# A GEGLU feed-forward kernel on one core: second-half data staged in single steps, x stored later, GpSimd held once

The change has five parts: sums of w_down staged by single steps with T2 in T1's place, x slices stored later, the first weight sums of the second half kept in the wd ring (with GpSimd held back once), two more warm-up matmuls, and the B21 loads called during M6.

## The chip, the cores and the metric

One core of one Trainium2 chip. The metric is the device time of one execution in microseconds (us), lower is better.

## The reference, cut to what matters

```python
# B, S, D, F = 1, 2048, 1024, 3584; all bf16
def reference(x, w_gate, w_up, w_down):
    return (gelu_tanh(x @ w_gate) * (x @ w_up)) @ w_down
```

## The kernel before

The rows of x are worked in two halves of 1024. Every 2x2 block product is done by a scheme with seven products in place of eight (M1 to M7), which needs sums of blocks: S sums of the left and T sums of the right operand. In the gate and up stage a "pair" (two chunks of 128 hidden columns, gate and up) takes 7 x 2 x 4 = 56 matmuls of 128x512. GpSimd makes the S sums for the next pair, ScalarE moves PSUM banks and does the gelu, VectorE adds M5 to other banks (`add_m5`), multiplies gate and up, and in the first half also does staging work: it makes T2 and T4 of w_down and SyncE stores them in HBM (`t_dram`), since there is room for only a part of them. SyncE also transposes slices of the second half's x and stores them in HBM (`x_dram`). All of these lie in order on their engines' queues.

```python
wd_pool = tile_pool("wd", bufs=3)     # w_down rows, later B21
o_pool  = tile_pool("o",  bufs=4)     # staging sums, x slices, gelu and output tiles

def stage_sums(i):                    # behind M4, for one or two i per pair
    w = staged[i]
    tt = [o_pool.tile([P, DN], F32R, name="o_sb") for _ in range(3)]   # T1, T2, T4
    for t, (in0, in1) in zip(tt, ops):
        dve(nc.vector.tensor_tensor(out=t[:], in0=in0, in1=in1, op=ALU.subtract))
    for j in range(2):                # store T2 and T4
        sp(nc.sync.dma_start(out=t_dram[:, j, i, :], in_=tt[1 + j][:].bitcast(F32)))

def stage_x(tb, kd):                  # behind M5, twice per pair, pairs 2 to 9
    t = o_pool.tile([P, 1, TB], BF16, name="o_sb")
    sp(nc.sync.dma_start_transpose(out=t[:], in_=xv[t0 : t0 + TB, kd : kd + 1, :]))
    sp(nc.sync.dma_start(out=x_dram[:, kd : kd + 1, ...], in_=t[:]))
...  # order inside a pair: M1, M5, M6, M2, M7, M3, M4; `then[...]` runs behind a product
    at = [min((pair - first_pair + d) * 4 // 3, NS) for d in range(3)]
    then["m5"] = [lambda q=q: stage_x(*q) for q in xs[:2]]
    then["m2"] = [lambda i=i: stage_load(i) for i in range(at[1], at[2])]
    then["m4"] = [lambda i=i: stage_sums(i) for i in range(at[0], at[1])]
...  # end of the first half: sums for the second half's first pair, on VectorE
    then1["m3"] = [t_sum("t1"), s_fill(0, "s1", "s2"), s_fill(1, "s1", "s2")]
    then1["m4"] = [a22 (ScalarE), b22 (ScalarE), t_sum("t2"), t_sum("t3"),
                   s_fill(0, "s3"), s_fill(1, "s3"), s_fill(0, "s4"), s_fill(1, "s4"),
                   t_sum("t4"), ...]                                   # shortened
```

## Time and profile before

| | before |
|---|---|
| median of the first three runs, us | 550.91 (550.12 to 553.39) |
| profiled run: whole, span, us | 554.47, 552.7 |
| TensorE busy | 539.6 us, 98% of the span |
| longest waits of TensorE | 4.4 and 1.4 us, both for VectorE's m5 addition |

TensorE is the bound and is almost never idle, so the table is read for what is left: two gaps. The prediction shows the lines. One more view: the waits of SyncE in the first half (who waited, for what: us in total, times, longest).

```profile
SPq L568 <- DMA o_sb<-in_x_dram: 43.1, 16, 6.4
SPq L553 <- DVE o_sb L549: 35.3, 17, 10.3
```
Line 568 is the store of an x slice, and its wait is for the slice's transpose to land: SyncE stood still for it 16 times, 43.1 us in all. Line 553 is the store of a T sum.

### The profile page before, as it was taken

Reading aid. Unit: us, or ns where it says so; the run is one execution under the profiler, and the core shown is the slowest. Engines: PE = TensorE matmul, PEld = TensorE weight load, DVE = VectorE, ACT = ScalarE, POOL = GpSimd, SP = SyncE. Lnnn points to the kernel's source line nnn. Section 1 sums busy time; section 2 is a strip of 40 time slices with the busy share of each in tenths; the row PEclk is TensorE's granted clock in tenths of the full one; section 3 lists DMA queues with packets and bytes.
Section 4 is the critical chain, followed back from the end, with each engine's and each line's share of the span. In section 5 each row is a group of like instructions: output and inputs, shape, how many; then the busy total and the mean of one; then the engine's idle time right before and its main releaser. Section 6 shows DMA issues by size and latency. Waiting matters only on the chain.

```text
span 552.7 us, 7222 instructions
## 1 busy us (share of the span) xinstructions
PE 539.6 (98%) x2373; PEld 375.9 (68%) x2409; DVE 355.1 (64%) x465; ACT 259.3 (47%) x434; POOL 243.0 (44%) x206
## 2 busy tenths in 40 slices
PE   8999999988999999999998999999999999999997
PEld 4457677755777767768676777766777676866765
DVE  0735677567686799789396444444444459979851
ACT  2425554444545516414564455555555552462270
POOL 0367777784778100000038677776777730000000
PEclk9999999998999999999999999999999999999999
DMA  9735576667695689769970413314040447767845
GB/s 272 222 109 161 175 229 215 159 198 232 183 328 189 219 313 364 260 209 323 300 272 1 152 37 117 94 60 151 2 153 0 154 137 238 274 210 246 280 144 204
DMA packets 81669, 104.82 MB, mean 190 GB/s; under 512 B 16608, under 2 KB 63200, under 8 KB 81632
## 3 DMA queue, kind: packets, MB, share of 16 engines
q1 hardware_dynamic: 81088, 103.83, 58.3%
q10 hardware_dynamic: 544, 0.52, 0.3%
q8 instruction: 20, 0.33, 0.3%
q14 instruction: 17, 0.14, 0.1%
HBM read 87.56 MB, written 13.63 MB: 183 GB/s over the span
## 4 chain that ended last, share of the span: by engine, by line
PE 87%; DMA 8%; DVE 3%; issue 1%; POOL 0%; SPq 0%; ACT 0%; DVEq 0%; ACTq 0%
PE bank L377 52%; PE bank L616 29%; PE bank L233 5%; DMA o_sb<-in_x_dram 4%; DMA t_mem<-t_dram 3%; DMA w_mem<-in_x_dram 1%; DVE s_mem L349 1%; DVE o_sb L549 1%; DMA x_dram<-o_sb 1%; DVE bank L400 1%; PE bank L295 1%; POOL s_mem L351 0%; DVE t_mem L222 0%; DVE t_mem L224 0%; DVE t_mem L227 0%
## 5 line engine op out<-in xcount | busy, mean ns | idle before, releaser
L377 PE MATMUL bank<-t_mem,s_mem 128*128 128x512 f32 x1040 | 257.3, 401 | 5.8 <-DVE bank L400 5.8
L377 PEld LDWEIGHTS bank<-t_mem,s_mem 128*128 128x128 f32 x1040 | 196.4, 189 | 52.2 <-issue 4.8
L351 POOL TENSOR_TENSOR s_mem<-w_mem 128x512 fp32r<-128x512 bf16 x100 | 118.4, 1203 | 200.2 <-DMA w_mem<-in_w_up_dram 107.0
L616 PE MATMUL bank<-t_mem,s_mem 128*128 128x512 f32 x560 | 130.4, 392 | 0.3 <-DMA t_mem<-t_dram 0.3
L400 DVE TENSOR_TENSOR bank<-bank,m 128x512 f32<-128x512 f32 x104 | 71.4, 696 | 80.1 <-ACT bank L420 72.8
L616 PEld LDWEIGHTS bank<-t_mem,s_mem 128*128 128x128 f32 x560 | 105.1, 188 | 23.4 <-DVE t_mem L526 0.7
L256 DVE TENSOR_TENSOR hT<-w_mem,bank 128x512 bf16<-128x512 f32 x104 | 71.0, 686 | 51.7 <-ACT w_mem L251 23.8
L251 ACT ACTIVATE w_mem<-bank 128x512 f32<-128x512 f32 x104 | 61.4, 596 | 89.7 <-DVE bank L400 58.8
L377 PE MATMUL bank<-xT,w_mem 128*128 128x512 bf16 x391 | 97.7, 380 | 1.3
L377 PEld LDWEIGHTS <-w_mem 128*128 128x128 bf16 x416 | 36.6, 98 | 50.5 <-issue 13.3
L526 DVE TENSOR_TENSOR t_mem<-w_mem 128x1024 fp32r<-128x1024 bf16 x56 | 65.5, 1217 | 0.0
L351 POOL TENSOR_TENSOR s_mem<-s_mem,w_mem 128x512 fp32r<-128x512 f32 x50 | 65.3, 1326 | 0.0
L351 POOL TENSOR_TENSOR s_mem<-w_mem,s_mem 128x512 fp32r<-128x512 bf16 x50 | 60.9, 1242 | 4.5 <-PE bank L377 4.5
L364 ACT CAST s_mem<-w_mem 128x512 fp32r<-128x512 bf16 x52 | 31.9, 615 | 28.0 <-PE bank L377 27.1
L591 DVE TENSOR_TENSOR s_mem<-hT 128x512 fp32r<-128x512 bf16 x56 | 37.5, 701 | 9.1 <-PE bank L616 7.0
L616 PEld LDWEIGHTS <-hT 128*128 128x128 bf16 x224 | 21.3, 98 | 26.6 <-issue 2.1
L415 ACT COPY m<-bank 128x512 f32<-128x512 f32 x52 | 30.6, 589 | 17.2 <-PE bank L377 17.0
L420 ACT COPY bank<-bank 128x512 f32<-128x512 f32 x52 | 29.6, 570 | 17.1 <-PE bank L377 17.1
L411 ACT COPY bank<-bank 128x512 f32<-128x512 f32 x52 | 29.5, 571 | 13.4 <-PE bank L377 13.4
L664 ACT CAST o_sb<-bank 128x512 bf16<-128x512 f32 x28 | 15.4, 586 | 39.9 <-PE bank L616 39.9
L233 PE MATMUL bank<-xT,w_mem 128*128 128x512 bf16 x125 | 29.0, 391 | 0.2
L549 DVE TENSOR_TENSOR o_sb<-wd_sb,o_sb 128x512 fp32r<-128x512 bf16 x28 | 23.8, 849 | 6.4 <-DMA x_dram<-o_sb 5.5
(37 smaller groups left out, 236.3 us busy)
## 6 DMA issues: line engine op xcount, KB each, us to landing
t_mem<-t_dram SPq DMA_DIRECT2D x56, 512.0 KB, 5.2
w_mem<-in_w_gate_dram SPq DMA_DIRECT2D x11, 1024.0 KB, 5.7
w_mem<-in_w_up_dram SPq DMA_DIRECT2D x11, 1024.0 KB, 8.4
wd_sb<-in_w_down_dram SPq DMA_DIRECT2D x28, 256.0 KB, 3.2
t_dram<-o_sb SPq DMA_DIRECT2D x28, 256.0 KB, 3.3
wd_sb<-in_w_down_dram SPq DMA_DIRECT2D x12, 512.0 KB, 8.7
w_mem<-in_w_down_dram SPq DMA_DIRECT2D x10, 512.0 KB, 6.6
w_mem<-in_w_down_dram SPq DMA_DIRECT2D x4, 1024.0 KB, 7.0
```

The costliest lines, as they stand in the source:

```text
L233: return nc.tensor.matmul(ps[:], lhsT=w_sb[:, kd, fi * P : (fi + 1) * P], rhs=xT[:, kd, tb * TB : (tb + 1) * TB], start=(kd == 0), stop=(k ...
L251: act(nc.scalar.activation(out=g_sb, in_=ps[:], func=ACT.Gelu_apprx_tanh))
L256: nc.vector.tensor_tensor(out=hT[:, fc, tb * TB : (tb + 1) * TB], in0=g_sb, in1=ps[:], op=ALU.mult,)
L351: pool(nc.gpsimd.tensor_tensor(out=t, in0=in0, in1=in1, op=op))
L364: act(nc.scalar.copy(out=t, in_=a(1, 1)))
L377: nc.tensor.matmul(banks[bank][:], lhsT=lhs[:, c, :], rhs=rhs[:, c, :], start=start and c == 0, stop=c == KH - 1, skip_group_check=True,)
L400: nc.vector.tensor_tensor(out=banks[dst][:], in0=banks[src][:], in1=m5[j][:], op=ALU.add)
L415: act(nc.scalar.copy(out=m5[j][:], in_=banks[VB[j]][:]))
L420: act(nc.scalar.copy(out=banks[RB[j]][:], in_=banks[QB[j]][:]))
L526: dve(nc.vector.tensor_tensor(out=t, in0=in0, in1=in1, op=ALU.subtract))
L591: dve(nc.vector.tensor_tensor(out=t, in0=in0, in1=in1, op=op))
L616: nc.tensor.matmul(banks[bset[u]][:], lhsT=lhs(i, u), rhs=rhs(i), start=start and i == 0, stop=stop and i == NS - 1, skip_group_check=True,)
```

## The change

Its intent: VectorE's staging bursts and waits out of the way of the m5 additions; less VectorE work where the second half begins; fewer conflicts with GpSimd; T2 loads not slowed by B21; the clock open earlier. The core of the diff:

```diff
-    NWARM = 9
+    NWARM = 11
     def pool(inst):
+        if "pool_wait" in last_on:          # a real wait for VectorE's last instruction
+            tc.add_manual_dep(inst.ins, last_on.pop("pool_wait").ins.name, SYNC_DEP, ...)
+        if on_dve and name in ("s1", "s2", "s3"):
+            if j == 0:
+                first_s[name] = wd_pool.tile([P, WDT, D], BF16, name="wd_sb")
+            t = first_s[name][:, j, :].bitcast(F32R)
-    def stage_sums(i):   # three buffers, three subtractions, two stores
+    def stage_step(n):   # one subtraction; T1 and T4 take a buffer, T2 is written over T1
+        i, k = n // 3, n % 3
+        if k != 1:
+            staged[i].append(o_pool.tile([P, DN], F32R, name="o_sb")[:])
     def stage_x(tb, kd):
         ... dma_start_transpose(...)
-        sp(nc.sync.dma_start(out=x_dram[...], in_=t[:]))
+        staged_x.append((x_dram[...], t[:]))       # stored by store_x()
-                at = [min((pair - first_pair + d) * 4 // 3, NS) for d in range(3)]
+                n = [min(4 * (pair - first_pair + d), NSTEP) for d in range(3)]
+                then["m7"] = [store_x]
+                then["m3"] = steps[:1] + [loads]
+                then["m4"] = steps[1:]
             if 6 < pair < 11:
-                then["m3"] = [s_down(hT, 0, "s3", ...)]
+                then["m5"] += [s_down(hT, 0, "s3", ...)]
-        for q in range(4): load_b21(n, q)          # before M6
+            if i == 4: (the same four loads)       # inside M6
+            then1["m2"] = [s1, s1, s2, s2, s3, s3]  # both weights
+            then1["m3"] = [t_sum("t1")]
             then1["m4"] = [..., s4, s4, t_sum("t4"),
+                pool_behind_dve,
```

## The prediction

> **What bounds the kernel now.** I read the page's first part, the waits of TensorE, its timeline, then the other engines and the DMA queue in the two stretches where TensorE stood still.
>
> ```profile
> PE 539.6 (98%) x2373; PEld 375.9 (68%) x2409; DVE 355.1 (64%) x465; ACT 259.3 (47%) x434; POOL 243.0 (44%) x206
> ```
> ```profile
> PE bank L377 <- DVE bank L400: 5.8, 2, 4.4
> PE bank L295 <- DMA w_mem<-in_x_dram: 0.9, 1, 0.9
> ...
> PE bank L616 <- DMA t_mem<-t_dram: 0.3, 1, 0.3
> ```
> TensorE is the bound: 539.6 of 552.7 us. Only four waits lie inside the run, and two of them, both for the VectorE addition of m5 (line 400), make 5.8 us. A wait costs more than its gap, so I measure it by the period of a pair of hidden blocks (56 matmuls), taken from windows that start at equal points of three pairs:
>
> ```profile
> 100.82:113.42 12.60, 12.55 (x56) 8.92 (x57) 8.36 (x12) 6.76 (x13) 9.09 (x8) 1.00 0.42 112
> 113.42:132.07 18.65, 14.24 (x56) 9.91 (x56) 13.15 (x17) 6.76 (x13) 10.92 (x8) 0.91 0.75 229
> ...
> 283.00:297.27 14.27, 12.83 (x55) 8.78 (x56) 13.66 (x14) 7.73 (x15) 11.85 (x8) 1.00 0.30 104
> ```
> The columns are the window, its length, then busy time and count of PE, PEld, DVE, ACT and POOL, the granted clock and the DMA's share and rate. An undisturbed pair takes 12.60 us; pair 8 took 18.65 (6.05 too many), the first pair of the second half 14.27 (1.67 too many). In pair 8 the gap is 4.36 us; the other 1.7 us is the half clock afterwards (126.10 to 129.51 was granted 0.50). The wait for T2 in the last group adds 0.5 us (one matmul start came 690 ns after the one before, usual 227). All three together: 8.2 us. That is everything the change can win outside the start.
>
> The cause in pair 8 stands on VectorE, whose queue is in order:
>
> ```profile
> 115.75 0.69 DVE L549 TENSOR_TENSOR o_sb<-wd_sb 128x512 fp32r<-128x512 bf16 x1 [1.38 <-DMA t_dram<-o_sb]
> ...
> 118.91 0.69 DVE L549 TENSOR_TENSOR o_sb<-wd_sb,o_sb 128x512 fp32r<-128x512 bf16 x1 [0.89 <-DMA x_dram<-o_sb]
> 121.83 1.58 DVE L549 TENSOR_TENSOR o_sb<-wd_sb 128x512 fp32r<-128x512 bf16 x1 [2.23 <-DMA x_dram<-o_sb]
> 123.45 2.25 DVE L549 TENSOR_TENSOR o_sb<-wd_sb,o_sb 128x512 fp32r<-128x512 bf16 x2
> 125.61 1.29 DVE L400 TENSOR_TENSOR bank<-bank,m 128x512 f32<-128x512 f32 x2
> ```
> Six staging subtractions (line 549) take buffers from the ring of four that the x slices use too. Three of them waited for a store to land (4.5 us), and the m5 addition of the next pair came at 125.61, where ScalarE's copy had been ready at 118.3.
>
> In the second half's first pair VectorE is late without waiting:
>
> ```profile
> 285.99 3.22 DVE L349 TENSOR_TENSOR s_mem<-w_mem,s_mem 128x512 fp32r<-128x512 bf16 x2
> 289.13 3.24 DVE L227 TENSOR_TENSOR t_mem<-xT,t_mem 128x2048 fp32r<-128x2048 bf16 x1
> ```
> ```profile
> 285.42 3.24 POOL L351 TENSOR_TENSOR s_mem<-w_mem 128x512 fp32r<-128x512 bf16 x2 [103.15 <-DMA w_mem<-in_w_up_dram]
> 288.62 4.77 POOL L351 TENSOR_TENSOR s_mem<-s_mem,w_mem 128x512 fp32r<-128x512 f32 x2
> ```
> Two sums took 3.22 us against 1.29 for the two just before, t4 took 3.24 against 2.29, and two GpSimd sums 4.77 against 2.27 elsewhere, exactly while both engines ran.
>
> **What the skill says.** (1) The Trainium skill, "SBUF — State Buffer", section "Who interferes with whom": VectorE's second port pair is GpSimd's, held by one of them for a whole instruction. The trace agrees: the numbers just given. (2) "TensorE: Matmul & The Clock Gate", Part 1: the clock opens or halves by free-running windows of 3413 ns. The half-clock stretch of this trace is 3.41 us long. Part 4 of that page says that a transpose doesn't count as busy in the same way; nothing here tests it. (3) "DMA: Bandwidth & Descriptors", "Anatomy of one DMA": most of a transfer's fixed 2 us is the receipt of the last write. Here a 128 KB x store takes 1.7 us at the median, so a reused x buffer is not free before that, however early it is wanted.
>
> **The change, part by part.**
>
> *Single steps, T2 in T1's place.* The work stays: 42 subtractions of about 0.7 us. Buffers fall from 3 to 2 per column pair of w_down, the pieces from up to 6 at the end of a pair to one behind M3 and three behind M4. A burst is then 3 x 0.7 = 2.1 us; it begins some 0.7 us into the next pair and ends by 2.9, and the m5 addition is wanted at 4.9. The first step falls into VectorE's idle 1.3 us before the last product (at 99.5 in the trace), beside GpSimd's s4, so it may take 1.5 us and push that product by 0.2: hidden.
>
> *x slices stored later.* The order was transpose, wait, store, transpose, wait, store, in which SyncE stood 43 us in total waiting for x to land. Now both transposes are issued, and both stores behind M7. But counting the ring of four through the new order (two x, then A, B by steps), the last step behind M4 still takes the buffer of the same pair's first x slice in pairs 2, 4, 5, 7 and 8. In 5 and 7 no weights are loaded and x lands in time. In 4 and 8 the slice is queued behind 2 MB of weights: it landed 9.0 to 13.3 us after the weights were issued (126.15 to 135.18, 91.71 to 105.04). With the weights at 3 to 5 us of the pair, landing is at 13 to 17, the store 2 us on at 15 to 19, the step done by 20, the addition by 21. M3 of the next pair wants it at 12.6 + 9.0 = 21.6. So pair 8's 6.05 us should go, with a rest of 0 to 1.5 us there, the more as the s3 sums moved to m5 (0.7 to 1.1 us in pairs 7 to 10) now stand before that addition. I set a rest of 0.5.
>
> *First weight sums in the wd ring.* s1, s2 and s3 of both weights (6 x 0.69 us) move ahead to M2, into buffers that B21 frees there. The last needs the up weights (landed 271.6), so five sums end at about 275, when t1 starts anyhow (275.52, when M3 frees its place). From t1's end at 277.8, or from 280.4 if t2 really waits for the last T4 load: 2 x 2.3 (t2, t3) + 1.3 (s4) + 2.3 (t4), ending at 286 to 288.7, not at 292.3. GpSimd is held until then, so the port is not shared. The addition is wanted at 287.8 by ScalarE's copy, at 291.65 by TensorE. The 1.67 us go in either case. GpSimd begins at most 3 us later, and has 8 sums of 1.15 us in a pair of 12.6.
>
> *B21 during M6.* Between the old and the new place stand only VectorE sums; SyncE's own list (T2 loads, then B21) keeps its order. Expected: the B21 loads are issued within 0.5 us of now, nothing gained or lost; the 0.5 us of T2 stay about half the time: 0.25 won.
>
> *Eleven warm-up matmuls.* Two more of 427 ns fill 0.85 of the 0.90 us gap before x arrives at 5.62; they delay nothing. They raise the chance that a whole window is busy before x comes; then six matmuls at 427 ns instead of 227 (1.2 us) and some transposes run fast. With a free-running window I take a quarter to a third of the runs: 0.4 us on average.
>
> Sum: 6.05 + 1.67 + 0.25 + 0.4 - 0.5 = 7.9 us off the profiled run. That run took 554.47 us as timed, so 546.6. But the timed runs before were 550.12 to 553.39, median 550.91, up to 4 us below the profiled one: either their stall in pair 8 is shorter, or profiling costs something. If only the stall, the end stays at 546.6; if only the profiling (3.6), it is 543.0. I weigh the first a little more and take **545.3 us**, 1.0% less.
>
> **Rivals.** (a) *The ring wait comes back.* In pair 4 or 8 the last step waits for x, as worked out above, and with a weights backlog of 1.75 MB of wd loads and T stores before it the addition slips by 2 to 5 us. For it: x landed 13.3 us late in pair 6 before. Against it: pair 7 then had a 4.1 us VectorE wait and TensorE didn't stop. It would make 547 to 550. (b) *The stall is shorter in unprofiled runs*, so there is little to win: 547 to 548. For it: the spread of 3.3 us among three runs. (c) *VectorE and GpSimd collide more*, since a step now sits beside GpSimd's s4 in ten pairs: it would show as pair periods over 12.60 us, each 0.2 us making 2 us. Against it: the products in question have slack.
>
> **Range and chances.** Low end: no rest, profiling costs 3 us, the start warms early: 542.5. High end: rival (a) or (b): 548.5. A gain over 2% needs less than 540.1, but with all 8.2 us of stalls and 1.4 us at the start gone from a profiled 554.47 one is at 544.9; even with 3.6 us of profiling cost that is 541.3. So 2%. Slower over 2% would take a new stall of 11 us beyond those lost: 1%.
>
> **What would show it.** Right, if the waits of TensorE lose line 400 (5.8 us to under 1), pairs 8 and 14 take 12.6 us, the clock isn't halved in the middle, GpSimd's first sum of the second half starts after t4 and takes 1.15 us, and two s4 sums take 1.3 us. The staging steps' waits on x stores should shrink from 7.8 us to under 4. Wrong, if the m5 addition still comes late behind a step that waits for an x store, if pair periods grow, or if the loads of B21 move by more than 0.5 us.

## The result, and the profile after

The changed kernel took 544.95 us (544.53 to 545.8, four runs), the kernel before 550.51 (549.76 to 553.39) in the same rounds: ratio 0.9894, 95% interval 0.9861 to 0.9928. A ratio here is the mean time of one kernel's runs over that of the other's of the same rounds, so not quite the ratio of the medians that are quoted.

The changed kernel's page and all waits of TensorE:

```profile
PE 537.7 (99%) x2411; PEld 374.1 (69%) x2411; DVE 349.5 (64%) x465; ACT 259.8 (48%) x434; POOL 242.2 (45%) x206
```
```profile
PE bank L204 <- PEq L912: 0.8, 1, 0.8
PE bank L244 <- DMA w_mem<-in_w_up_dram: 0.4, 1, 0.4
PE bank L306 <- DMA w_mem<-in_x_dram: 0.3, 1, 0.3
```
All three lie in the first 8 us. From there on TensorE never waited. The periods of pair 8 and of the second half's first pair (columns as in the prediction):

```profile
111.75:124.35 12.60, 12.60 (x58) 8.93 (x57) 9.71 (x14) 6.88 (x13) 10.18 (x9) 1.00 1.04 322
...
275.00:287.60 12.60, 12.60 (x57) 8.93 (x56) 9.83 (x11) 7.88 (x14) 7.55 (x7) 1.00 0.37 124
```
Both are 12.60 us now, and the clock is 1.00 in both. VectorE from the end of pair 8 on:

```profile
124.94 1.41 DVE L570 TENSOR_TENSOR o_sb<-wd_sb,o_sb 128x512 fp32r<-128x512 bf16 x2
127.13 1.38 DVE L570 TENSOR_TENSOR o_sb<-wd_sb 128x512 fp32r<-128x512 bf16 x1 [0.79 <-DMA x_dram<-o_sb]
128.43 1.65 DVE L607 TENSOR_TENSOR s_mem<-hT 128x512 fp32r<-128x512 bf16 x1
130.00 1.28 DVE L419 TENSOR_TENSOR bank<-bank,m 128x512 f32<-128x512 f32 x2
```
One step stands behind M3 (122.95, 0.68 us) and three behind M4 (line 570), the last of which still waits for an x store, as the prediction counted; but it waits 0.79 us, and the m5 additions (line 419) are in time. Where the second half begins, VectorE and GpSimd:

```profile
276.49 1.28 DVE L368 TENSOR_TENSOR s_mem<-w_mem,wd_sb 128x512 fp32r<-128x512 bf16 x2
277.69 2.28 DVE L238 TENSOR_TENSOR t_mem<-xT,t_mem 128x2048 fp32r<-128x2048 bf16 x1
280.12 0.70 DVE L419 TENSOR_TENSOR bank<-bank,m 128x512 f32<-128x512 f32 x1
```
```profile
280.05 2.27 POOL L370 TENSOR_TENSOR s_mem<-w_mem 128x512 fp32r<-128x512 bf16 x2 [104.99 <-DVE t_mem L238]
```
The two s4 sums take 1.28 us and t4 2.28 us, where they took 3.22 and 3.24; GpSimd starts behind t4. And SyncE in the first half:

```profile
SPq L572 <- DVE o_sb L570: 51.6, 22, 10.7
SPq L586 <- DMA o_sb<-in_x_dram: 18.5, 9, 4.7
```
Its waits for x fell from 43.1 to 18.5 us. Its waits for T sums rose meanwhile, from 35.3 to 51.6: the queue still stands, but behind the x slices less, so what lies behind those leaves earlier.

The spans differ by 10.0 us, 552.7 against 542.7. The terms, read off the two traces: pair 8 6.05, the first pair of the second half 1.67, the wait for T2 0.46, the start 1.67 (the second group of transposes begins at 10.90 instead of 12.57 us): 9.85 us. The medians differ by 5.6 only, because the profiled run of before was one of its slow ones: its 33 runs were between 547.68 and 554.71 us. The changed kernel's ten runs (six of them as the run `u_b21` below) were between 544.51 and 545.8.

The stall was not special to the profiled run. Each of the 33 runs has its mean granted clock on record: in 25 it was 0.993 to 0.997, and these took 550.22 to 554.71 us; in the other eight it was 0.999 or 1.000, and these took 547.68 to 550.16. One half-clock stretch like that of the trace lowers the mean by 3.41 x 0.5 / 552.7 = 0.003, so by this estimate most runs had a stall long enough to halve the clock once or twice. The changed kernel's ten runs have 0.999 or 1.000. For runs without a trace this is read from the clock alone; where they stalled is not shown.

### The profile page after: what moved, and what is told of

Its sections match the earlier page's. It is cut to its first block, busy times and chain, and to the rows that moved or that the text cites. A ratio compares the mean times of both kernels' runs of the same rounds, so it can differ in the third digit from the quotient of the medians.

```text
span 542.7 us, 7261 instructions
## 1 busy us (share of the span) xinstructions
PE 537.7 (99%) x2411; PEld 374.1 (69%) x2411; DVE 349.5 (64%) x465; ACT 259.8 (48%) x434; POOL 242.2 (45%) x206
## 4 chain that ended last, share of the span: by engine, by line
PE 98%; DMA 1%; ACT 0%; ACTq 0%; issue 0%
PE bank L396 60%; PE bank L632 32%; PE bank L244 5%; DMA w_mem<-in_w_up_dram 1%; PE bank L306 0%; ACT o_sb L680 0%; ACTq L167 0%; ACTq L680 0%
## 5 line engine op out<-in xcount | busy, mean ns | idle before, releaser
L396 PE MATMUL bank<-t_mem,s_mem 128*128 128x512 f32 x1016 | 249.2, 399 | 0.0
L396 PEld LDWEIGHTS bank<-t_mem,s_mem 128*128 128x128 f32 x1016 | 190.9, 188 | 44.2
L370 POOL TENSOR_TENSOR s_mem<-w_mem 128x512 fp32r<-128x512 bf16 x100 | 120.9, 1230 | 196.1 <-DVE t_mem L238 105.0
L632 PE MATMUL bank<-t_mem,s_mem 128*128 128x512 f32 x560 | 130.1, 392 | 0.0
L632 PEld LDWEIGHTS bank<-t_mem,s_mem 128*128 128x128 f32 x560 | 105.2, 188 | 22.7
L370 POOL TENSOR_TENSOR s_mem<-w_mem,s_mem 128x512 fp32r<-128x512 bf16 x50 | 63.3, 1288 | 0.0
L370 POOL TENSOR_TENSOR s_mem<-s_mem,w_mem 128x512 fp32r<-128x512 f32 x50 | 59.3, 1206 | 0.0
L607 DVE TENSOR_TENSOR s_mem<-hT 128x512 fp32r<-128x512 bf16 x56 | 40.5, 754 | 10.5 <-PE bank L632 7.0
L542 ACT CAST t_mem<-w_mem 128x1024 fp32r<-128x1024 bf16 x28 | 26.9, 1048 | 0.0
```

Of the source, the lines that this page charges most:

```text
L370: pool(nc.gpsimd.tensor_tensor(out=t, in0=in0, in1=in1, op=op))
L396: nc.tensor.matmul(banks[bank][:], lhsT=lhs[:, c, :], rhs=rhs[:, c, :], start=start and c == 0, stop=c == KH - 1, skip_group_check=True,)
L607: dve(nc.vector.tensor_tensor(out=t, in0=in0, in1=in1, op=op))
L632: nc.tensor.matmul(banks[bset[u]][:], lhsT=lhs(i, u), rhs=rhs(i), start=start and i == 0, stop=stop and i == NS - 1, skip_group_check=True,)
```

## The experiments

Twelve kernels ran, six timed runs each, in three calls, each beside eleven runs of the kernel before, whose mean was 551.40, 551.69 and 551.82 us in the three. "Over" is the mean against 545.15 us, the mean of `u_b21`, whose instructions are those of the changed kernel.

| run | edit | median (range), us | ratio to before | mean over changed |
|---|---|---|---|---|
| u_b21 | changed, B21 called at the old place | 545.21 (544.51 to 545.56) | 0.9888 | 0 |
| u_stage | changed, whole staging undone | 548.08 (545.82 to 550.59) | 0.9944 | 3.1 |
| u_fill | changed, first sums and hold undone | 546.56 (546.29 to 548.83) | 0.992 | 1.8 |
| u_warm | changed, nine warm-ups | 545.76 (545.0 to 546.3) | 0.9899 | 0.6 |
| u_xstore | changed, x stored at once | 549.52 (546.03 to 551.85) | 0.9949 | 3.9 |
| u_three | changed, T2 in its own buffer | 544.93 (544.57 to 545.76) | 0.9876 | -0.1 |
| u_burst | changed, bursts of whole columns | 546.14 (545.74 to 546.91) | 0.99 | 1.1 |
| o_xown | before, x in a buffer of its own | 554.71 (552.71 to 555.21) | 1.0046 | 9.2 |
| o_late | before, x stored later | 548.74 (548.1 to 550.03) | 0.9945 | 3.7 |
| o_min | before, x stored later, GpSimd held | 547.1 (546.19 to 548.01) | 0.9916 | 2.0 |
| u_fillhold | changed, first sums undone, hold kept | 544.95 (544.56 to 546.29) | 0.9882 | 0.1 |
| u_hold | changed, without the hold | 546.04 (545.61 to 546.99) | 0.9896 | 1.0 |

The 95% intervals of the ratios are 0.002 to 0.004 either way, mostly from the scatter of the kernel before.

**Each part undone: u_stage, u_fill, u_warm, u_b21.**

u_stage puts back `stage_sums`, the immediate x store, the old schedule and the s3 sums behind M3.

> The changed kernel with the staging of the first half put back: bursts of three or six subtractions behind M4 with three buffers each, each x slice stored at once, s3 sums behind M3. Theory A (ring waits of the staging are the larger part): 2.5 to 5 us over the changed kernel (about 548 to 550), VectorE waits for x stores of 5 us or more in the first half, and a TensorE gap for the m5 addition of over 1 us about pair 8. Rival B (that stall was special to one profiled run; the gain is in the second half's first pair and the start): at most 1.5 us over the changed kernel, no TensorE gap over 0.5 us in the first half.

Measured: 3.1 us over, and a TensorE gap of 2.1 us at 120.5 us, in pair 8. Theory A holds for the part as a whole; the waits for x stores were 4.3 us, less than expected. The profiled run, 547.01 us, is one of its faster ones: its gap explains the 1.9 us of that run, and the slower runs were not traced.

u_fill:

```diff
-            then1["m2"] = [s1, s1, s2, s2, s3, s3]
-            then1["m3"] = [t_sum("t1")]
+            then1["m3"] = [t_sum("t1"), s1, s2, s1, s2]
-            (first_s tiles of the wd ring)   +  (their old place in s_mem)
-                pool_behind_dve,
```

> The changed kernel with the first weight sums of the second half put back into the shared buffer behind M3 and M4, and without holding GpSimd. Theory A: 1.7 us over the changed kernel (1.2 to 2.2), one TensorE gap of about 1.4 us for the m5 addition in the first pair of the second half, t4 at 3.2 us and two s4 sums at 3.2 us. Rival B: the same gap and at least half of the whole gain, 2.7 us or more.

Measured: 1.8 us over (median 1.35), one gap of 1.39 us in that pair, t4 3.24 us, two s4 sums 3.21 us. As expected.

u_warm:

```diff
-    NWARM = 11 ... b = banks[i % 8]
+    NWARM = 9  ... b = banks[max(i - 1, 0)]
```

> The changed kernel with nine warm-up matmuls. Theory A: 0 to 0.8 us over the changed kernel on average, its runs scattered by up to 1.6 us according to where the clock's window falls. Rival C: the two matmuls decide whether the clock opens before x arrives, and are worth 1.2 us or more in every run.

Measured: 0.6 us over, inside theory A's range. The trace's clock records say when the full clock was first granted: among the nine profiles with eleven warm-ups always by 6.4 us (4.3 to 6.4); among the five with nine at 4.4, 4.7, 9.0, 9.6 and 10.0 us. u_warm's own trace shows why, by the two windows of 3.41 us that end where the clock opened (length, TensorE busy and count first; the clock column reads 1.00 because the records begin at the opening):

```profile
2.19:5.60 3.41, 2.60 (x8) 0.61 (x6) 0.00 (x0) 0.92 (x1) 0.00 (x0) 1.00 0.92 310
5.60:9.01 3.41, 3.41 (x21) 2.27 (x22) 0.72 (x2) 1.38 (x2) 0.00 (x0) 1.00 1.10 352
```
The first window had the gap before x in it, was busy for 2.60 of 3.41 us, and did not open the clock; the next, all busy, did. The same reckoning fits all fourteen profiles: the 3.41 us before the opening were busy for 3.32 us or more, and the 3.41 us before those for 2.72 at the most. Eleven warm-ups close that gap, or leave up to 0.7 us of it where the clock had opened during the warm-ups. So rival C is nearer than I allowed: not every run gains, but three of these five opened late; five are few for a rate.

u_b21:

```diff
+        for q in range(4):
+            load_b21(n, q)
         done("m5")
...
-            if i == 4:
-                for q in range(4):
-                    load_b21(n, q)
```

> The changed kernel with the B21 loads called where they were, before M6. Its instruction lists were compared with those of the changed kernel and are the same on every engine but for buffer numbers, so every theory expects 0, within 0.4 us: this run shows the noise of such a comparison.

Measured: 545.21 us, the changed kernel's 544.95 within 0.3. Its profile has a 0.28 us wait for T2 in the last group, which the changed kernel's lacks: with equal programs that is chance. This part of the change does nothing.

**What in the staging counts: u_xstore, u_three, u_burst, o_xown.** The prediction blamed the ring of four and bursts; these four take the parts of the staging apart.

u_xstore:

```diff
-        staged_x.append((x_dram[...], t[:]))
+        sp(nc.sync.dma_start(out=x_dram[...], in_=t[:]))
-                then["m7"] = [store_x]
```

> The changed kernel with each x slice stored at once again (transpose, store, transpose, store), all else as changed. Theory A1 (smaller pieces and fewer buffers do it, the later stores nothing): 0 to 0.5 us over the changed kernel, no TensorE gap in the first half. Theory A2 (SyncE standing behind each x slice is what holds the ring): 1.5 us or more over it, with a TensorE gap in the first half.

Measured: 3.9 us over, no less than the whole staging undone, with a TensorE gap of 1.6 us in the first half. Theory A2 holds. The profiled run, 547.0 us, was again one of the faster (546.03 to 551.85), so its gap shows the kind of stall, not the whole 3.9. Its SyncE waits for x are back:

```profile
SPq L583 <- DMA o_sb<-in_x_dram: 40.5, 16, 5.3
```

u_three:

```diff
-        if k != 1:
-            staged[i].append(o_pool.tile(...))
+        staged[i].append(o_pool.tile(...))      # T1, T2 and T4 each their own
```

> The changed kernel with T2 in a buffer of its own: three buffers of the ring per column pair, single steps and late x stores kept. A pair of blocks then takes six buffers of a ring of four, so in all pairs with x slices two steps behind M4 wait for x stores of the same pair. Theory A1: 0.5 to 2.5 us over the changed kernel and VectorE waits for x stores of 6 us or more. If T2's place does nothing: 0 to 0.4 us and waits as now (about 2 to 5 us).

Measured: 0.1 us under the changed kernel, VectorE waits for x stores of 0.6 us, no TensorE gap in the pairs. A1's expectation is a clear miss: T2 in T1's place is worth nothing here, beside single steps and late stores; without these it was not tried. The 0.6 itself says little: six profiles with the staging of the changed kernel, unedited, had 2.2 to 6.2 us of such waits.

u_burst:

```diff
-                n = [min(4 * (pair - first_pair + d), NSTEP) for d in range(3)]
+                n = [3 * min((pair - first_pair + d) * 4 // 3, NS) for d in range(3)]
-                then["m3"] = steps[:1] + [loads] ; then["m4"] = steps[1:]
+                then["m3"] = [loads]             ; then["m4"] = steps
```

> The changed kernel with whole columns again, three or six subtractions in one burst behind M4, but with T2 in T1's place and late x stores. Theory A1: 0.5 to 2.5 us over the changed kernel, with a TensorE gap after pairs with six subtractions. If only the buffers count: 0 to 0.4 us.

Measured: 1.1 us over, one gap of 1.09 us after pair 7, which has six subtractions. VectorE there, with no wait for a store at all:

```profile
114.50 1.65 DVE L570 TENSOR_TENSOR o_sb<-wd_sb 128x512 fp32r<-128x512 bf16 x1
116.19 3.10 DVE L570 TENSOR_TENSOR o_sb<-wd_sb,o_sb 128x512 fp32r<-128x512 bf16 x2
...
120.79 1.28 DVE L419 TENSOR_TENSOR bank<-bank,m 128x512 f32<-128x512 f32 x2
```
GpSimd begins its sums at 114.31. The three subtractions before that took 0.7 us each, these three 1.6, and the s3 sum left out here 1.65. So a burst costs here by running on past GpSimd's idle 2.7 us, not by its buffers.

o_xown:

```diff
+    x_pool = ctx.enter_context(tc.tile_pool(name="xs", bufs=1))
-        t = o_pool.tile([P, 1, TB], BF16, name="o_sb")
+        t = x_pool.tile([P, 1, TB], BF16, name="x_sb")
```

> The kernel before with one buffer of their own for the x slices, so that no staging subtraction can wait for an x store; nothing else is changed. Theory A (those waits cause the stall of pair 8): VectorE's waits for x stores are gone from the staging line, and the run is 2 to 4 us shorter than before. Rival D (the queue of SyncE is late anyway and the wait moves to the T stores): at most 1 us shorter, with as much waiting for T stores.

Measured: 2.7 us longer than before (554.36 against 551.69, means). No subtraction waits for an x store any more, yet the stall stays. VectorE at pair 8:

```profile
116.77 1.64 DVE L550 TENSOR_TENSOR o_sb<-wd_sb,o_sb 128x512 fp32r<-128x512 bf16 x1 [2.29 <-DMA t_dram<-o_sb]
118.34 1.64 DVE L550 TENSOR_TENSOR o_sb<-wd_sb 128x512 fp32r<-128x512 bf16 x1
```
The wait moved to the T stores (rival D), because these stand behind x in SyncE's queue; with one x buffer SyncE also waits for each x store, another 11.6 us. And a late subtraction falls beside GpSimd and takes 1.64 us instead of 0.69. Theory A's forecast of 2 to 4 us less is a miss. But the single x buffer brought a wait of its own, so this run alone does not clear the shared ring; `u_three` and `u_fillhold` say more about it.

How far SyncE's queue was behind is seen in the issue times of the x transposes. Counted from the start of their pair (the first copy of an M1 bank less 0.9 us), the first slice of pairs 3 to 8 was issued at

| | 3 | 4 | 5 | 6 | 7 | 8 |
|---|---|---|---|---|---|---|
| before | 3.4 | 4.3 | 8.1 | 5.2 | 10.7 | 14.2 |
| changed | 2.6 | 4.2 | 6.0 | 4.1 | 3.2 | 4.8 |
| u_xstore | 2.6 | 4.2 | 7.7 | 7.1 | 9.5 | 7.6 |
| u_three | 2.6 | 4.2 | 4.4 | 4.2 | 3.4 | 5.0 |
| o_late | 3.3 | 4.4 | 10.7 | 5.1 | 4.1 | 9.4 |

us of a pair of 12.6. In the kernel before, pair 8's slice was issued after pair 8 should have ended. In `o_late`, the first run below, slices are late after the two bursts of pairs 4 and 7, but the queue catches up between them. Two stretches of SyncE's timeline, of pair 7, show it; first before, then changed:

```profile
105.06 0.34 SPq L568 DMA_DIRECT2D x_dram<-o_sb  x1
105.44 1.12 SPq L563 DMA_TRANSPOSE o_sb<-in_x_dram  x1
...
108.44 1.87 SPq L535 DMA_DIRECT2D wd_sb<-in_w_down_dram  x4
110.36 0.90 SPq L553 DMA_DIRECT2D t_dram<-o_sb  x2
111.31 1.90 SPq L563 DMA_TRANSPOSE o_sb<-in_x_dram  x1
```
```profile
98.29 0.82 SPq L586 DMA_DIRECT2D x_dram<-o_sb  x2
99.16 0.46 SPq L572 DMA_DIRECT2D t_dram<-o_sb  x1
99.67 0.93 SPq L556 DMA_DIRECT2D wd_sb<-in_w_down_dram  x2
100.70 1.40 SPq L572 DMA_DIRECT2D t_dram<-o_sb  x2
102.14 3.26 SPq L581 DMA_TRANSPOSE o_sb<-in_x_dram  x2
```
Before, the slices of pair 6 are stored at 105.06 and 108.06, one landing after the other, then come pair 6's loads and T stores, and only then, at 111.31, pair 7's first slice. Changed, both slices of pair 6 land together and pair 7's leave at 102.14.

**Is the late store enough, and what is it in the second stall: o_late, o_min, u_fillhold, u_hold.**

o_late is the kernel before with `store_x` behind M7 (the `stage_x` part of the diff above and the line `then["m7"] = [store_x]`), nothing else.

> The kernel before with one thing of the change: x slices are stored behind M7, so SyncE issues both transposes, the w_down loads and only then waits for x. Bursts, three buffers, everything else as before. Theory A2 (SyncE standing behind each x slice is what makes the stall of pair 8): 2.5 to 4.5 us shorter than before, SyncE's wait for x falls from 43 us to about 20, the staging's waits for stores to under 3 us. If bursts and buffers are needed as well: at most 1.5 us shorter.

Measured: 3.0 us shorter than before (means 548.84 and 551.82). SyncE's wait for x fell to 9.1 us, far below the 20 expected, and its wait for T sums rose to 65.6; the staging's waits for x stores were 3.3 us, a little over what was expected. A gap of 2.1 us remains, now after pair 4, which has six subtractions: there a wait of 1.73 us pushes four of them beside GpSimd. That is u_burst's effect again. The waits of TensorE and SyncE:

```profile
PE bank L377 <- DVE bank L400: 3.5, 2, 2.1
```
```profile
SPq L553 <- DVE o_sb L549: 65.6, 25, 10.3
SPq L570 <- DMA o_sb<-in_x_dram: 9.1, 6, 2.2
```
The second of the two TensorE waits, 1.4 us, is the stall of the second half, which this run leaves in.

o_min adds the hold:

```diff
                 lambda: t_sum("t4"),
+                pool_behind_dve,
```

> The kernel before with two edits only: x stored behind M7, and GpSimd's first sum of the second half held until t4 is done. Theory A2 with contention as the cause of the second stall: 1.4 to 1.8 us shorter than the run with the late stores alone, so 4 to 6 us shorter than before and within 1.5 us of the changed kernel; no TensorE gap in the first pair of the second half.

Measured: 1.6 us shorter than o_late (means), 4.6 shorter than before, no gap in the first pair of the second half. To the changed kernel it lacked 2.0 us, not 1.5: it still has the bursts (a gap of 0.95 us after pair 4) and nine warm-ups, and in its profile the wait for T2 happened to be 0.63 us.

u_fillhold is u_fill with `pool_behind_dve` kept.

> The changed kernel with the first weight sums of the second half back in the shared buffer behind M3 and M4, but GpSimd held until t4 is done. Theory E (the collision with GpSimd makes the 1.4 us gap): VectorE's chain then ends near 290 in the time of the kernel before, 1.5 us ahead of TensorE's need, no gap, 0 to 0.4 us over the changed kernel. Theory F (six sums too many in the chain make it): the gap stays at 1 us or more.

Measured: 0.1 us over, no gap. VectorE keeps all six sums where they were:

```profile
278.54 1.29 DVE L362 TENSOR_TENSOR s_mem<-w_mem,s_mem 128x512 fp32r<-128x512 bf16 x2
279.75 2.29 DVE L238 TENSOR_TENSOR t_mem<-xT,t_mem 128x2048 fp32r<-128x2048 bf16 x1
```
The m5 addition follows at 281.95. In u_fill the same three began at 278.52, 281.66 and 284.82, with 3.21 and 3.24 us for the sums. The two programs differ in the hold alone, so the collision made the stall (theory E), and the hold alone cures it.

u_hold is the changed kernel without that one line.

> The changed kernel without the hold on GpSimd, the first sums still moved ahead. GpSimd's sums for the second pair no longer wait for M5 (s1 of the first pair lies elsewhere), so they start some 10 us earlier, beside t1, t2, t3, s4 and t4 on VectorE. Theory E: these slow each other, t4 ends 3 to 5 us later, 0.5 to 2 us over the changed kernel with a TensorE gap for the m5 addition. Theory F: 0 to 0.4 us, no gap.

Measured: 1.0 us over, a gap of 0.44 us. GpSimd now started at 263.4, and VectorE's s2 and s3 sums took 1.6 us each, t1 3.25:

```profile
266.28 3.23 DVE L368 TENSOR_TENSOR wd_sb<-wd_sb,w_mem 128x512 fp32r<-128x512 f32 x2
...
272.58 3.25 DVE L230 TENSOR_TENSOR t_mem<-xT 128x2048 fp32r<-128x2048 bf16 x1
```
The gap explains less than half of the 1.0 us (0.4); between jobs 0.3 us is noise, and the rest stays open. Moving the sums ahead is not needed with the hold; without it the move lets GpSimd start 14.5 us earlier than in u_fill (277.95). By the program that is because the first pair's s1 no longer lies in the buffer it writes; no run isolates it.

No version tried is faster than the changed kernel: u_three and u_fillhold equal it within the noise.

## Why the prediction was right or wrong

The time, 545.3 us forecast and 544.95 measured, was right. Its steps fared differently.

- **Pair 8 and the first pair of the second half at 12.60 us, the clock never halved, GpSimd behind t4 at 1.15 us a sum, s4 at 1.3 us for two.** All right. The term for the second stall, 1.67 us, was measured as 1.8 by undoing (u_fill) and 1.6 by adding the hold (o_min against o_late).
- **"Six staging subtractions take buffers from the ring of four that the x slices use too."** The lines are true, and in that trace the 4.5 us of waits are the last link: the addition came at 125.61, TensorE had stood since 122.09. What failed is the number of buffers as the thing to change. Giving x its own buffer made the kernel slower (o_xown), giving T2 one cost nothing (u_three), and u_fillhold, as fast as the changed kernel, waited 6.2 us for x stores, nearly the 7.8 of before. What counts is when x is stored: 3.0 us by that alone. How it works is read from the traces, not isolated: SyncE stood behind each x slice, so the stores and loads in its queue slipped, and with them the buffers. I had the 43 us before me and did not give them a share.
- **Single steps against late stores.** The 6.05 us were not divided between them. The runs do, each part with the others as they were: late stores 3.0 us added to before, 3.9 taken from the changed kernel; single steps 1.1 and T2's place 0, both taken from the changed kernel.
- **The first step beside GpSimd's s4 "may take 1.5 us".** It took 0.68; the two s4 sums took 2.83 us instead of 2.30, so GpSimd paid. The s3 sums moved behind M5 took 1.65, not 0.7 to 1.1. Both had slack.
- **A rest of 0.5 us in pair 8, rival (a).** No gap there. The slice landed 10.2 us after the weights were issued (115.00 to 125.24), in the lower part of the range I gave, and the weights went out at 3.5 us of the pair.
- **First sums in the wd ring.** t4 ended at 280.0, which is 288.0 in the time of the kernel before (its pair began 8.0 us later), inside the 286 to 288.7 worked out; but the move is not what won the time, the hold is.
- **B21: order of SyncE's queue kept.** Right: instructions are equal, and counted from the ScalarE copy 4.2 us earlier the loads leave as in the kernel before. The quarter us won "half the time" was wrong: 0.
- **Warm-up 0.4 us.** 0.6 measured. The share of runs that gain was mis-sized: I took a quarter to a third, the profiles give three of five with nine against none of nine with eleven that opened late.
- **"Either their stall in pair 8 is shorter, or profiling costs something."** The first is what the record points to: the profiled run of the changed kernel, 544.53, is as fast as its others, and the kernel before scatters over 7 us by itself, with the clock on record falling as the time grows. I took 1.3 us off for a cost of profiling that the changed kernel does not show, and gave the start 0.4 where the two profiled runs differ by 1.67. That these two errors cancel is luck, and so is part of how near the time came: 554.47 - 6.05 - 1.67 - 0.46 - 1.67 = 544.62, and the rest of 0.5 us and half of the T2 wait put the forecast 0.7 us above that.

Undone one at a time, the parts give 3.1 + 1.8 + 0.6 + 0 = 5.5 us, and the difference of the means is 6.5 (551.64 less 545.15). The last us is within the scatter of the kernel before and of u_stage, or an interplay; it was not settled.

## What to carry to other kernels

A queue that issues transfers in order and waits for one to land holds up everything behind it; issue all the transfers first, and put the stores that depend on them where the data has landed. Before giving a late instruction more buffers, look at what the issuing queue stood behind, and by how much it slips from one round to the next; the sum of its waits tells little, since they moved to other work here. And where VectorE and GpSimd both read SBUF, keep VectorE's extra work in GpSimd's idle time, or hold GpSimd once: one added wait was as good as moving six sums.

## What the Trainium skill lacked or had wrong

- "TensorE: Matmul & The Clock Gate", Part 4, says that transposes do not count as busy in the same way for the clock. The 32 transposes here are of that mode. In u_warm the window 5.60 to 9.01 us was filled by transposes for its first half (from 5.58 to the first matmul at 7.26), and the clock opened at its end, while a window with 76% of matmuls and an idle rest did not open it. Counted without transposes, the window that opened the clock would have been the emptier one. Here they counted.
- The same page, Part 1, gives no busy share that a window needs. Here 2.72 of 3.42 us (80%, o_late) did not open the clock, and 3.32 of 3.41 us (97%, u_three) did; between these no run tells.
- "SBUF — State Buffer", "Who interferes with whom", says that of VectorE and GpSimd the second one to issue waits for the first, but its two slowdowns stand without shapes, and it has none for two streams side by side. Here VectorE's subtraction of 128x512 went from 0.69 to 1.64 us and GpSimd's sum from 1.15 to about 1.6 us: both lose. For single instructions the order decides, as the page has it: in the changed kernel a step begun at 122.95 kept its 0.68 us, and GpSimd's sum of 122.97 took 1.70 instead of 1.15; in u_xstore a sum begun at 85.47 kept 1.17 us, and the step of 85.52 took 1.67.
- "DMA: Bandwidth & Descriptors" does not say how long the issue of a DMA transpose holds the queue with transfers ahead of it: 1.12 us at the least in the kernel before, 5.40 us behind 2 MB of weights.
